# Shorter v loads with copies by VectorE, earlier transposing transfers, and more unread products at the start

## The chip, the cores and the metric

The kernel runs on one core of a Trainium2 chip. A core has a matrix engine (TensorE, PE in the profile), VectorE (DVE), ScalarE (ACT), GpSimd (POOL) and SyncE (SP), each with an instruction stream of its own that runs in order, and 16 DMA engines that they share. Matrix products write to PSUM, everything else lies in SBUF. The metric is the device time of one execution in microseconds; a time given for a kernel is the median of several runs, and a profile is one execution.

## The reference, cut to what matters

Chunked attention with a little memory, followed by a gated network. B, H, S, D = 4, 8, 768, 64; the queries of a sequence are cut into 24 chunks of 32, and each chunk sees 16 keys before it, its own 32, 8 after it and 8 memory keys.

```
for c in range(24):
    l, r = max(0, 32*c - 16), min(768, 32*c + 40)
    keys   = concat(mem_k, k[:, :, l:r]);  vals = concat(mem_v, v[:, :, l:r])
    s      = (q_c @ keys.T) / sqrt(64);    a = softmax(s)
    out[:, :, 32*c:32*c+32] = a @ vals
x = out.transpose(0, 2, 1, 3).reshape(3072, 512)
y = (maximum(x @ w_gate, 0) * (x @ w_val)) @ w_out      # d_ff = 1536
```

Inputs are float32 in DRAM, the result is 3072 x 512 float32. Inside, the kernel works in bf16 and f16.

## The kernel before, in words

**Tiles.** A tile is 128 queries of one batch (four chunks) with all eight heads: 24 tiles, six to a batch (`TPB`). The attention of tile a: transpose its q and k (L275, operations "t"), copy them out of PSUM ("tc"), scores (L309, 32 small products), row maximum and subtraction on VectorE, exponent on ScalarE, sum, reciprocal and normalisation on VectorE, transpose the probabilities (L358, "p") and copy them out ("pc"), then the products with the values (L388, "v"; L374 and L381 in batch 0) and a copy to xT ("x"). The network works on blocks of 2, 2, 2, 4, 4, 4, 4 and 2 tiles (`BLOCKS`): 12 pieces of w_gate and w_val (L407, "f"), ReLU on ScalarE (L413), product on VectorE (L419), then w_out (L432, "o") and a store.

**Transposes by transfer.** From tile `LATE_QK` on, q and k are transposed by DMA transfers that SP issues (L283); q lands in place, k in a buffer k_t that is then copied. From tile `LATE_P` on the same holds for the probabilities (L362). Both are 18 here, that is, batch 3.

**v.** In batch 0, v is loaded as it lies (v_n) and moved to the chunks' places by products with a shifted identity (L215, "sh") and copies. For the other batches v_bd[b % 2] holds, for each of 4 head pairs and 24 chunks, a 128 x 128 matrix: two heads on the diagonal, for each 56 rows of context and 8 of memory. So v_bd must be zero off the diagonal. Its context rows are loaded straight from DRAM with a cast (`load_v_rows`, L184): row s of chunk c is key 32c + s - 16, so 56 rows for each chunk, and the rows 32 to 55 of a chunk are the rows 0 to 23 of the next one, loaded a second time. Two loads a batch, one for each half of the heads; the last one of batch 3 is cut in two. The memory rows are copied in by small DMAs ("mr", L167), by SP in batch 1 and by GpSimd after. v_bd[1] is zeroed at the start by VectorE and ScalarE ("z1"). Parts of v_bd[0] serve batch 0 as v_q and vmem_f; it is zeroed by GpSimd ("z", L135), in the queue of its loads, after the values of tile 5.

**GpSimd** issues all casting loads in one fixed order (the list `loads`): q and k pairs and v of batch 0, weights, then the q and k tiles and v of later batches, mr among them.

**The order of the work** is made by a planner in the kernel (`schedule`). Each operation has engines with planned durations, dependencies, a priority, and buffers that it takes and gives; the planner steps through planned time and writes down one list, and each engine then runs its part of it in order. FFN evictions have priority 0, attention 1, network products on PE 2. `pace` and `pace_t` hold transposes of later tiles back.

**Unread products.** From planned 1.3 to `WARM` = 16 us, whenever PE has nothing ready, the planner puts in a product of zeros that nobody reads (`idle_product`, L140), planned at 0.107 us up to 6 us and 0.056 after. It writes to a buffer of the pool `fps` (four PSUM buffers, used by shifts and by the network), which is given back at planned 16.1 us. The scores take their PSUM tile anew for each tile from `sps`, a pool of one buffer.

Of the kernel before, what the change touches and what calls it, by code (L numbers as in the profile page):

```python
# [9 lines left out]
F32 = mybir.dt.float32  # L10
# [4 lines left out]
ACT = mybir.ActivationFunctionType  # L15
# [4 lines left out]
def kernel(  # L20
# [12 lines left out]
    nc = tc.nc  # L33

    B, H, S, D = q.shape
# [15 lines left out]
    BLOCKS = [2, 2, 2, 4, 4, 4, 4, 2]  # L51
    GROUPS = [(0, 2), (2, 6), (6, 9), (9, 12)]
    BAND0 = 48

    LATE_QK, LATE_P = 18, 18

    KEY_RUNS = ((0, CH, 0), (KW, 64, CH), (CH, KW, CTX))
    assert sum(BLOCKS) == NT and NMEM == 8 and D == 64 and H == 8
# [67 lines left out]
            moe_w_out.rearrange("(c p) f -> p c f", p=128)[:, n * i:n * i + n, :],  # L126
        )

    def zero(eng, t, hp):
        x = t[:, hp].bitcast(F32)  # L130
        if eng is nc.scalar:
            z = idle.bitcast(F32)
            nc.scalar.copy(x, bass.AP(tensor=z.tensor, offset=z.offset, ap=[z.ap[0], [0, NCH], [1, D]]))
        else:
            eng.memset(x.rearrange("p c d -> p (c d)"), 0.0)  # L135

    def idle_product(N):
        if "idle" not in TMP:
            TMP["idle"] = fps.tile([128, 512], F32, tag="fps", name="idle_ps")
        nc.tensor.matmul(TMP["idle"][:, 0:N], lhsT=idle, rhs=idle[:, 0:N], start=True, stop=True)  # L140


    def mem_load():
# [45 lines left out]
    def v_parts(b, par, c0, c1):  # L189
        parts = []  # L190
        if (b, par, c1) == (B - 1, 1, HP * NCH):
            c1 -= 1
            parts.append((b, par, 0, 48, c1, c1 + 1))
        return parts + [(b, par, 0, CTX, c0, c1)]


    def load_v_tile(t):
# [98 lines left out]

    def scores(a):
        b, t = divmod(a, TPB)
        s = sps.tile([128, 2, 512], F32, name="s_ps")
        keys = kT[b].rearrange("p h c s -> p h (c s)")  # L300
        for h2 in range(HP):
            m, par = h2 % 2, h2 // 2
            for g in range(4):
                c = 4 * t + g
                lo, hi = max(KW * c - 16, 0), min(KW * c + 48, NCH * KW)
                o0 = 64 * (2 * m + par) + lo - (KW * c - 16)
                for r in range(2):
                    d = slice(D * r, D * r + D)
                    nc.tensor.matmul(s[CH * g:CH * g + CH, r, o0:o0 + hi - lo],  # L309
                                     lhsT=qT[b][d, h2, CH * c:CH * c + CH],  # L310
                                     rhs=keys[d, h2, lo:hi], start=True, stop=True)
        S_ps[a] = s.rearrange("p a (h s) -> p a h s", s=64)[:, :, 0:HP, :]
# [155 lines left out]
    op("idle", {"DVE": 0.2}, lambda e: nc.vector.memset(idle, 0.0), prio=(-10,))  # L468
    for hp in range(HP):
        op(("z1", hp), {"DVE": 1.5, "ACT": 1.6}, lambda e, hp=hp: zero(engine[e], v_bd[1], hp), ["idle"], prio=(-1, hp), after=["warm2", "vmem_f"] + ["ib"] * (hp > 0))  # L470
    op("warm", {"DVE": 0.15}, lambda e: nc.vector.memset(warm, 0.0), prio=(-9,))  # L471
    op("warm2", {"ACT": 1.5}, lambda e: nc.scalar.activation(warm, warm, ACT.Exp), ["warm"], prio=(-9,))
    op("vmem_f", {"DVE": 0.55}, lambda e: nc.vector.memset(vmem_f, 0.0), prio=(-8,), after=["warm"])
# [42 lines left out]
    for a in range(NT):  # L516
# [41 lines left out]
        if b == 0:  # L558
# [46 lines left out]
    def load_qk_op(a, i):  # L605
        load(("qk", a, i), 1024, 1.05, lambda: load_qk(a, i), take=["qk"])

    def load_v_op(b, half, par, c0, c1, n, deps, after):
        for i, part in enumerate(reversed(v_parts(b, par, c0, c1))):
            rows = part[3] - part[2]  # L610
            load(("vl", b, half, n) if i == 0 else ("vx", b, n), rows * (part[5] - part[4]),
                 rows * (part[5] - part[4]) * 1.15e-3, lambda part=part: load_v_rows(*part), deps, (), after)
# [6 lines left out]
    def load_zero(s, hp):  # L619
        load(("z", s, hp), 0, 1.5, lambda: zero(nc.gpsimd, v_bd[s], hp), [("v", TPB - 1)])  # L620

    def load_pair_op(r, i):
        load(("pl", r, i), 1024, 1.45, lambda: load_pair(r, i))
# [25 lines left out]
    for i in range(2):  # L649
        load(("wo", i), 768, 4.1, lambda i=i: load_out(i))  # L650
    for b in range(1, B):
        deps = ([("z", 0, HP - 1)] if b > 1 else [("z1", hp) for hp in range(HP)]) + ([("v", TPB * (b - NSET + 1) - 1)] if b > NSET else [])
        if b == 1:
            for n in range(2 * HP):
                op(("mr", b, n), {"SP": 0.72}, lambda e, n=n: mem_rows(nc.sync, 1, n),
                   deps + [(("vm", 0), 0.2), (("vm", 1), 0.2)], (0,))
        for par in range(2):
            load_v_op(b, 0, par, 0, HP * NCH, par, [], deps)
# [12 lines left out]
    def timed(d):  # L671
        return isinstance(d, tuple) and len(d) == 2 and isinstance(d[1], float)
# [1 line left out]
    def schedule():  # L674
        done, started, times = {}, set(), [0.7]
        free = {e: 0.7 for e in ("PE", "ACT", "DVE", "SP", "POOL")}
        queue_end, flying, gives = 0.0, [], [(WARM + 0.1, "fps")]
        room["fps"] -= 1
        heapq.heappush(times, WARM + 0.1)
# [26 lines left out]
        while len(started) < len(ops) + len(loads):  # L706
# [8 lines left out]
            while moved:  # L715
                moved = False
                for e in ("POOL", "PE", "ACT", "DVE", "SP"):
                    if free[e] > t + 1e-9:
                        continue
                    if e == "POOL":  # L720
                        if n_load == len(loads):
                            continue
                        o = loads[n_load]
                        if len(flying) >= 8 or not ready(o, t):
                            continue
                        n_load += 1
                        key = o["key"]
                        if o["n"]:
                            end = t + 0.62 + 0.27e-3 * o["n"]
                            queue_end = max(queue_end, end + 0.8) + o["work"]  # L730
                            flying.append(queue_end + 1.0)
                            done[key] = queue_end + (1.2 if n_load < 8 else 2.4 if n_load < 45 else 6.0 if key[0] == "vl" else 4.0)
                        else:
                            end = done[key] = t + max(o["work"], 0.6)
                        fn = o["fn"]
                    else:
                        o = None
                        for _, key in todo[e]:
# [4 lines left out]
                            alone = len(ops[key]["eng"]) == 1 or e == "ACT"  # L743
                            if e != "PE" and 6.0 < t < HASTE and alone and ready(ops[key], t + 0.4):
                                break
# [70 lines left out]
```

## Time and profile before

| | |
|---|---|
| median of 3 runs | 248.03 us (247.85 to 248.07) |
| the profiled execution | 248.07 us |
| its span, first to last instruction | 246.3 us |
| mean granted TensorE clock | 0.993 |
| busy PE, DVE, ACT, POOL | 238.8, 139.8, 115.9, 85.4 us |
| first network product begins | 24.09 us |
| unread products | 138, the last ending at 16.9 us |
| v loads of batches 1 to 3 (L184) | 7 issues, 13.9 us of POOL, 17.3 us from issue to landing in the middle |
| zeros by GpSimd | 4 of 1.42 us, from 75.2 us |
| transposing transfers by SP | 18, from 109.98 us |

How to read it: a row of a view names the line of the kernel, the engine, what it writes and reads, and how often, then busy time and mean duration. "[0.87 <-issue]" behind an instruction of the timeline says that its engine sat idle 0.87 us before it, and what ended that; "issue" means that the profile shows nothing that it waited for. Matmuls overlap each other, so the spacing of two starts says more than a duration. A line number such as L78 or L80 is that of a helper that copies for many operations. The DMA share is of 16 engines and can exceed 1 where transfers overlap.

### The profile page before, as it was taken

Reading aid. Unit: us, or ns where it says so; the run is one execution under the profiler, and the core shown is the slowest. Engines: PE = TensorE matmul, PEld = TensorE weight load, DVE = VectorE, ACT = ScalarE, POOL = GpSimd, SP = SyncE. Lnnn points to the kernel's source line nnn. Section 1 sums busy time; section 2 is a strip of 40 time slices with the busy share of each in tenths; the row PEclk is TensorE's granted clock in tenths of the full one; section 3 lists DMA queues with packets and bytes.
Section 4 is the critical chain, followed back from the end, with each engine's and each line's share of the span. In section 5 each row is a group of like instructions: output and inputs, shape, how many; then the busy total and the mean of one; then the engine's idle time right before and its main releaser. Section 6 shows DMA issues by size and latency. Waiting matters only on the chain.

```text
span 246.3 us, 6675 instructions
## 1 busy us (share of the span) xinstructions
PE 238.8 (97%) x2811; PEld 146.5 (59%) x2811; DVE 139.8 (57%) x271; ACT 115.9 (47%) x259; POOL 85.4 (35%) x101
## 2 busy tenths in 40 slices
PE   7988998999999999999999999999999999999994
PEld 7776887886579645555445545455445444444873
DVE  5475868886278438796048779999342034320430
ACT  5665545754466334643235575765332232312432
POOL 8975689305289950398901420000000000000000
PEclk9998999999999999999999999999999999999999
DMA  7999999999999699399999594361101210002102
GB/s 75 174 180 204 201 158 184 175 138 84 168 202 135 37 159 130 26 132 141 181 198 144 24 109 85 110 148 27 21 3 45 85 43 0 0 33 97 43 3 85
DMA packets 109757, 25.77 MB, mean 105 GB/s; under 512 B 100768, under 2 KB 106656, under 8 KB 109728
## 3 DMA queue, kind: packets, MB, share of 16 engines
q0 software_dynamic: 94368, 16.42, 105.2%
q10 hardware_dynamic: 3600, 6.29, 7.5%
q1 hardware_dynamic: 11760, 2.64, 7.4%
q8 instruction: 22, 0.36, 0.6%
q14 instruction: 7, 0.06, 0.1%
HBM read 32.06 MB, written 6.29 MB: 156 GB/s over the span
## 4 chain that ended last, share of the span: by engine, by line
PE 93%; ACT 2%; issue 2%; DVE 1%; POOL 1%; ACTq 0%; DVEq 0%; POOLq 0%
PE v_ps L407 25%; PE out_ps L432 25%; PE g_ps L407 25%; PE xT_ps L388 3%; PE idle_ps L140 3%; PE s_ps L309 2%; PE qk_ps L275 2%; PE pT_ps L358 2%; PE vs_ps L215 2%; PE xT_ps L381 2%; PE qk_ps L236 1%; ACT kT L78 1%; PE xT_ps L374 1%; POOL qk_p L227 1%; ACT v_bd L78 0%
## 5 line engine op out<-in xcount | busy, mean ns | idle before, releaser
L419 DVE TENSOR_TENSOR gvT<-v_ps,g_relu 128x256 f16<-128x256 f32 (+1 forms) x96 | 52.9, 554 | 54.8 <-PE v_ps L407 40.7
L407 PE MATMUL v_ps<-xT,w_val_sb 128*128 128x256 f16 (+1 forms) x384 | 78.5, 327 | 0.1
L407 PE MATMUL g_ps<-xT,w_gate_sb 128*128 128x256 f16 (+1 forms) x384 | 78.5, 327 | 0.0
L413 ACT ACTIVATE g_relu<-g_ps 128x256 f16<-128x256 f32 (+1 forms) x96 | 46.9, 490 | 55.6 <-PE g_ps L407 53.7
L432 PE MATMUL out_ps<-w_out_sb,gvT 128*128 128x512 f16 (+2 forms) x300 | 65.8, 371 | 0.0
L407 PEld LDWEIGHTS <-w_gate_sb 128*128 128x128 f16 x384 | 36.8, 98 | 24.1 <-issue 0.4
L407 PEld LDWEIGHTS <-w_val_sb 128*128 128x128 f16 x384 | 35.9, 98 | 21.2 <-issue 0.3
L432 PEld LDWEIGHTS <-gvT 128*128 128x128 f16 x300 | 28.0, 98 | 29.7
L78 ACT COPY o_sb<-out_ps 128x512 f32<-128x512 f32 (+2 forms) x25 | 14.2, 568 | 34.4 <-PE out_ps L432 26.3
L337 ACT ACTIVATE p_exp<-dif 128x256 f16<-128x256 f32 (+2 forms) x72 | 19.6, 339 | 9.5 <-DVE dif L329 9.4
L254 POOL DMA_DIRECT2D qk_b<-in_k_dram x18 | 16.4, 909 | 18.6 <-issue 9.9
L167 POOL DMA_DIRECT2D v_bd<-vmem x16 | 10.1, 638 | 27.9 <-DMA v_bd<-in_v_dram 18.3
L322 DVE TENSOR_REDUCE mx<-s_ps 128x8 f32<-128x512 f32 x24 | 16.5, 689 | 5.4 <-PE s_ps L309 5.0
L341 DVE TENSOR_REDUCE sm<-p_exp 128x8 f32<-128x512 f16 x24 | 16.3, 680 | 4.2 <-ACT p_exp L337 4.1
L329 DVE TENSOR_TENSOR dif<-s_ps,mx 128x512 f32<-128x512 f32 x24 | 16.5, 686 | 0.4
L254 POOL DMA_DIRECT2D qk_b<-in_q_dram x18 | 16.3, 906 | 1.1 <-PE qk_ps L275 0.5
L352 DVE TENSOR_TENSOR p_n<-p_exp,rinv 128x512 f16<-128x512 f16 x24 | 16.5, 686 | 0.3
L78 ACT CAST xT<-xT_ps 128x512 f16<-128x512 f32 x16 | 9.4, 585 | 11.6 <-PE xT_ps L388 8.8
L184 POOL DMA_DIRECT2D v_bd<-in_v_dram x7 | 13.9, 1997 | 1.9 <-issue 1.0
L388 PEld LDWEIGHTS <-v_bd 128*128 128x128 f16 x288 | 9.6, 96 | 3.6
L140 PE MATMUL idle_ps<-idle 128*128 128x128 bf16 x138 | 10.7, 240 | 1.0 <-DVE warm L471 1.0
L80 DVE COPY qT<-qk_ps 128x512 bf16<-128x512 bf16 x9 | 4.1, 455 | 11.9 <-PE qk_ps L275 11.8
(57 smaller groups left out, 177.2 us busy)
## 6 DMA issues: line engine op xcount, KB each, us to landing
out_dram<-o_sb ACTq DMA_DIRECT2D x23, 256.0 KB
v_bd<-in_v_dram POOLq DMA_DIRECT2D x5, 672.0 KB, 17.3
qk_b<-in_k_dram POOLq DMA_DIRECT2D x18, 128.0 KB, 7.1
qk_b<-in_q_dram POOLq DMA_DIRECT2D x18, 128.0 KB, 7.0
w_out_sb<-in_moe_w_out_dram POOLq DMA_DIRECT2D x2, 768.0 KB, 10.6
qk_p<-in_k_dram POOLq DMA_DIRECT2D x3, 256.0 KB, 5.4
qk_p<-in_q_dram POOLq DMA_DIRECT2D x3, 256.0 KB, 6.7
v_n<-in_v_dram POOLq DMA_DIRECT2D x6, 128.0 KB, 6.4
```

What stands on the lines that cost most here:

```text
L78: nc.scalar.copy(o, i)
L140: nc.tensor.matmul(TMP["idle"][:, 0:N], lhsT=idle, rhs=idle[:, 0:N], start=True, stop=True)
L254: nc.gpsimd.dma_start(qk_b[a, i], bass.AP(tensor=x.tensor, offset=x[b, 0, 128 * t, 0].offset, ap=[[D, 128], [S * D, H], [1, D]]))
L322: nc.vector.reduce_max(SM[a, "mx"], s4, axis=AX.X)
L329: nc.vector.tensor_tensor(out=SM[a, "dif"].rearrange("p (m r) a s -> p r m a s", r=2), in0=S_ps.pop(a).rearrange("p r (m a) s -> p r m a s ...
L337: nc.scalar.activation(p[:, :, :, s0:s0 + k1 - k0], dif[:, :, :, k0:k1], ACT.Exp, scale=SCALE)
L352: nc.vector.tensor_tensor(out=P_n[a], in0=SM.pop((a, "p")), in1=rinv_b, op=ALU.mult)
L388: nc.tensor.matmul(ps[:, hp, r], lhsT=v_bd[b % NSET][:, hp, 4 * t + g, :], rhs=x[:, hp, r], start=True, stop=True)
L407: nc.tensor.matmul(ps, lhsT=w[:, f, 128 * m:128 * m + 128], rhs=xTs[blk][:, f, :], start=(f == 0), stop=(f == NFC - 1))
L413: nc.scalar.activation(st["r", m], st.pop((0, m)), ACT.Relu)
L419: nc.vector.tensor_tensor(out=st["gv"][:, m, :], in0=st.pop((1, m)), in1=st.pop(("r", m)), op=ALU.mult)
L432: nc.tensor.matmul(st["o", t, c], lhsT=st["gv"][:, m, 128 * t:128 * t + 128], rhs=w_out_sb[:, m, c[0]:c[1]], start=(m == 0), stop=(m == ND ...
```

## The change

- The two v loads of a batch read 32 rows for each chunk instead of 56 ("vl"), and one more small load for each half of the heads brings the last 16 rows behind the last chunk ("ve"). Rows 32 to 55 of a chunk are copied on VectorE from rows 0 to 23 of the next chunk (`upper`, "up"): 24 partitions by at most 12 chunks of 64, eight copies for each three tiles (`UT`), 16 a batch, 48 in all. The values of tile t of a batch wait for the copies up to its third.
- The zeros of v_bd[0] are made by ScalarE or VectorE ("z0"): one head pair at the start, after v_bd[1]'s, and the other three in thirds of eight chunks; that of the last pair after vmem_f has been read, the two that hold v_q after the values of tile 5.
- `LATE_QK` and `LATE_P` go from 18 to 15: q, k and probabilities of tiles 15, 16 and 17 are transposed by transfers too, and their issue is held back by `pace_t`.
- Unread products fill planned gaps up to 22 us, planned at 0.107 us up to 9 us and 0.060 after. They write into an unused part of the second bank of the score tile, which is now one tile for the whole kernel, and no buffer of `fps` is held for them.

```diff
+    UT = 3
-    LATE_QK, LATE_P = 18, 18
+    LATE_QK, LATE_P = 15, 15
...
+    s_all = sps.tile([128, 2, 512], F32, name="s_ps")
     def idle_product(N):
-        if "idle" not in TMP:
-            TMP["idle"] = fps.tile([128, 512], F32, tag="fps", name="idle_ps")
-        nc.tensor.matmul(TMP["idle"][:, 0:N], lhsT=idle, rhs=idle[:, 0:N], start=True, stop=True)
+        nc.tensor.matmul(s_all[:, 1, 256:256 + N], lhsT=idle, rhs=idle[:, 0:N], start=True, stop=True)
...
+    def upper(b, par, i0, i1, eng):
+        x = v_bd[b % NSET].rearrange("p h c d -> p (h c) d")
+        d = slice(D * par, D * par + D)
+        copy(eng, x[64 * par + CH:64 * par + CTX, i0:i1, d], x[64 * par:64 * par + CTX - CH, i0 + 1:i1 + 1, d])
...
+    op(("z0", HP - 2), {"DVE": 1.5, "ACT": 1.6}, ..., ["idle"], prio=(-1, HP), after=["ib", ("z1", 0)])
+    for hp in (HP - 1, 0, 1):
+        for c0 in range(0, NCH, 8):
+            op(("z0", hp, c0), {"ACT": 0.6, "DVE": 0.55}, lambda e, hp=hp, c0=c0: zero(engine[e], v_bd[0], hp, c0, c0 + 8),
+               ["vm0" if hp == HP - 1 else ("v", TPB - 1)], prio=(3, -hp) if hp == HP - 1 else (0.7, hp), after=[("v", 3)])
...
-           + ([("vl", b, 0, n) for n in range(2)] if b else [("shc", 4 * t), ("shc", 4 * t + 2), "vm0"])
+           + ([("vl", b, n) for n in range(2)] + [("up", b, n, m) for n in range(2 * HP) for m in range(t // UT + 1)]
+              + [("ve", b, n) for n in range(2) if last] if b else [("shc", 4 * t), ("shc", 4 * t + 2), "vm0"])
...
+    def load_v_op(b, par, deps):
+        n = HP * NCH
+        load(("vl", b, par), CH * n, CH * n * 1.03e-3, lambda: load_v_rows(b, par, 0, CH, 0, n), (), (), deps)
+        load(("ve", b, par), 16, 0.05, lambda: load_v_rows(b, par, CH, CH + 16, n - 1, n), (), (), deps)
+    for b in range(1, B):
+        for n in range(2 * HP):
+            hp, par = divmod(n, 2)
+            for m in range(TPB // UT):
+                i0 = NCH * hp + 4 * UT * m
+                i1 = min(i0 + 4 * UT, HP * NCH - 1)
+                op(("up", b, n, m), {"DVE": 0.1 + 64 * 0.5e-3 * (i1 - i0)}, ...,
+                   [("vl", b, par)], (1, TPB * b - 1 + UT * m, 9), (), (), [("v", TPB * b - 7)] if b > 1 else [])
...
-        if b == 1:
-            for hp in range(HP):
-                load_zero(0, hp)
-    HASTE, WARM = 0.0, 16.0
+    WARM = 22.0
...
-        queue_end, flying, gives = 0.0, [], [(WARM + 0.1, "fps")]
-        room["fps"] -= 1
+        queue_end, flying, gives = 0.0, [], []
...
-                                free[e] = t + (0.107 if t < 6.0 else 0.056)
+                                free[e] = t + (0.107 if t < 9.0 else 0.06)
```

More of the change, by code (lines that the diff above doesn't have):

```diff
@@ L127, in load_out, with zero @@
         )
[L129 to L130 removed]
+    def zero(eng, t, hp, c0=0, c1=NCH):
+        x = t[:, hp, c0:c1].bitcast(F32)
         if eng is nc.scalar:
             z = idle.bitcast(F32)
[L133 removed]
+            nc.scalar.copy(x, bass.AP(tensor=z.tensor, offset=z.offset, ap=[z.ap[0], [0, c1 - c0], [1, D]]))
         else:
             eng.memset(x.rearrange("p c d -> p (c d)"), 0.0)
+    s_all = sps.tile([128, 2, 512], F32, name="s_ps")
     def idle_product(N):
[L138 to L140 removed]
+        nc.tensor.matmul(s_all[:, 1, 256:256 + N], lhsT=idle, rhs=idle[:, 0:N], start=True, stop=True)
     def mem_load():
@@ L298, in scores @@
         b, t = divmod(a, TPB)
-        s = sps.tile([128, 2, 512], F32, name="s_ps")
+        s = s_all
         keys = kT[b].rearrange("p h c s -> p h (c s)")
@@ L470 @@
         op(("z1", hp), {"DVE": 1.5, "ACT": 1.6}, lambda e, hp=hp: zero(engine[e], v_bd[1], hp), ["idle"], prio=(-1, hp), after=["warm2", "vmem_f"] + ["ib"] * (hp > 0))
+    op(("z0", HP - 2), {"DVE": 1.5, "ACT": 1.6}, lambda e: zero(engine[e], v_bd[0], HP - 2), ["idle"], prio=(-1, HP), after=["ib", ("z1", 0)])
+    for hp in (HP - 1, 0, 1):
+        for c0 in range(0, NCH, 8):
+            op(("z0", hp, c0), {"ACT": 0.6, "DVE": 0.55}, lambda e, hp=hp, c0=c0: zero(engine[e], v_bd[0], hp, c0, c0 + 8),
+               ["vm0" if hp == HP - 1 else ("v", TPB - 1)], prio=(3, -hp) if hp == HP - 1 else (0.7, hp), after=[("v", 3)])
     op("warm", {"DVE": 0.15}, lambda e: nc.vector.memset(warm, 0.0), prio=(-9,))
@@ L606, in load_qk_op @@
         load(("qk", a, i), 1024, 1.05, lambda: load_qk(a, i), take=["qk"])
[L608 to L612, printed above, removed]
+    def load_v_op(b, par, deps):
[8 more added lines that the diff above has]
+                i1 = min(i0 + 4 * UT, HP * NCH - 1)
+                op(("up", b, n, m), {"DVE": 0.1 + 64 * 0.5e-3 * (i1 - i0)},
+                   lambda e, b=b, par=par, i0=i0, i1=i1: upper(b, par, i0, i1, engine[e]),
+                   [("vl", b, par)], (1, TPB * b - 1 + UT * m, 9), (), (), [("v", TPB * b - 7)] if b > 1 else [])
     def load_w_op(g):
@@ L651 @@
     for b in range(1, B):
-        deps = ([("z", 0, HP - 1)] if b > 1 else [("z1", hp) for hp in range(HP)]) + ([("v", TPB * (b - NSET + 1) - 1)] if b > NSET else [])
+        deps = ([("z0", HP - 2)] + [("z0", hp, c0) for hp in (HP - 1, 0, 1) for c0 in range(0, NCH, 8)] if b > 1 else [("z1", hp) for hp in range(HP)]) + ([("v", TPB * (b - NSET + 1) - 1)] if b > NSET else [])
         if b == 1:
@@ L657 @@
         for par in range(2):
[L658 removed]
+            load_v_op(b, par, deps)
         if b > 1:
@@ L742, in schedule @@
                                 break
-                            alone = len(ops[key]["eng"]) == 1 or e == "ACT"
-                            if e != "PE" and 6.0 < t < HASTE and alone and ready(ops[key], t + 0.4):
-                                break
                         if o is None:
```

9 lines of the change are left out of this document (removed).

## The prediction

> **What bounds the kernel now.** I read the page's busy shares first, then its slices, the chain of waits, a table of windows, and last the instructions of PE in order of time.
>
> ```profile
> span 246.3 us, 6675 instructions
> PE 238.8 (97%) x2811; PEld 146.5 (59%) x2811; DVE 139.8 (57%) x271; ACT 115.9 (47%) x259; POOL 85.4 (35%) x101
> PEclk9998999999999999999999999999999999999999
> PE 93%; ACT 2%; issue 2%; DVE 1%; POOL 1%; ACTq 0%; DVEq 0%; POOLq 0%
> q8 instruction: 22, 0.36, 0.6%
> ```
>
> TensorE sets the end: 93% of the chain is its own work, and from 46 us on it waits for nobody. So a product removed after 46 us is worth its spacing, and whatever VectorE, ScalarE, GpSimd or the DMAs gain is worth nothing by itself. The fourth digit of the clock row is an 8: in the slice from 18.5 to 24.6 us the granted clock is down. The windows show how much (columns: stretch, length, busy time of PE, weight load, DVE, ACT, POOL, granted clock, DMA share, GB/s).
>
> ```profile
> 18.76:22.18 3.42, 2.55 (x105) 1.96 (x106) 1.62 (x4) 1.65 (x3) 1.87 (x4) 1.00 1.25 202
> 22.18:25.59 3.41, 3.41 (x46) 2.68 (x41) 2.47 (x5) 2.41 (x6) 1.79 (x3) 0.50 1.27 203
> 39.24:42.65 3.41, 2.70 (x62) 2.10 (x61) 3.37 (x6) 1.41 (x4) 3.41 (x3) 1.00 1.31 199
> ```
>
> A window in which PE was busy 2.55 of 3.42 us (75%) is followed by one at half clock in which PE never idles. Half of 3.41, 1.70 us, is lost there. The window with 2.70 (79%) had no such follower.
>
> Why was PE idle in the first? In order of time (start, length, instruction):
>
> ```profile
> 14.05 0.22 PE L309 MATMUL s_ps<-kT,qT 64*32 64x64 bf16 x7 [0.40 <-issue]
> 14.20 0.85 PE L215 MATMUL vs_ps<-v_n,band 128*64 128x256 f16 x12
> 14.98 1.91 PE L140 MATMUL idle_ps<-idle 128*128 128x128 bf16 x31
> 16.82 0.41 PE L236 MATMUL qk_ps<-ident_b,qk_p 128*64 128x128 bf16 x8
> 17.16 0.40 PE L358 MATMUL pT_ps<-band,p_n 128*128 128x128 f16 x4
> 18.05 0.41 PE L236 MATMUL qk_ps<-ident_b,qk_p 128*64 128x128 bf16 x8 [0.49 <-ACT qT L78]
> 18.40 0.40 PE L374 MATMUL xT_ps<-pT,vmem 128*128 128x128 f16 x4
> 18.73 0.68 PE L381 MATMUL xT_ps<-pT,v_bd 56*64 56x32 f16 x32
> 19.34 0.40 PE L358 MATMUL pT_ps<-band,p_n 128*128 128x128 f16 x4
> 19.66 0.26 PE L309 MATMUL s_ps<-kT,qT 64*32 64x64 bf16 x18
> 20.80 0.25 PE L309 MATMUL s_ps<-kT,qT 64*32 64x64 bf16 x14 [0.87 <-issue]
> ```
>
> Both "issue" stops fall in the middle of a tile's scores and wait for no engine. Between them lie 7+12+31+8+4+8+4+32+4+18 = 128 products, with their weight loads 256 instructions. The instruction queue moved 0.36 MB in 22 pieces, 16 KB each, which is 64 bytes for each of 256. So I read them as waits for the next block of PE's program. Blocks came 6.75 us apart here (14.05 to 20.80) while the DMAs are full: 53 ns a product.
>
> **The change part by part.**
>
> *Transposes of tiles 15 to 17.* PE loses three times the q and k transposes (eight products; 137.59 to the next one at 138.04: 0.45 us) and the transpose of P (153.62 to 153.84: 0.22). 3 x 0.67 = 2.0 us off the bound engine, about 125 to 155 us. Six evictions go (0.42 on DVE or 0.59 on ACT), three k copies stay, now from k_t (0.29 or 0.61). SP issues nine more transposing transfers, 1.19 to 1.31 us each, 11 us; it has nothing between its rows for v_bd, which end at 46.7, and 109.98. The q and k ones go ahead of tile 18's. Those of P are new among the q and k transfers of tiles 21 to 23 (144.10 to 153.2 now): a late q or k load holds SP, P of tile 15 stands behind it, and PE at tile 15's values behind that. Bounds: nothing, as for tiles 18 to 21, where P was ready at 155.97 and used at 161.40 with PE not waiting; up to 3.8 us, SP's longest wait for p_n. I take nothing, since tiles 18 to 21 are the same step.
>
> *v loads.* Each batch's two loads shrink from 56 to 32 rows of 96 chunks, 5376 to 3072 pieces, plus two of 16 pieces. POOL takes 2.2 us for 5376 and 0.9 for the 1024 of a q tile, so 1.5 for 3072 and 0.6 for a small one (24 KB rows of v_bd: 0.63): 4.2 us a batch against 4.4. The DMAs get some 13,700 of 94,368 packets less; PE waits for no DMA after 46 us, so: nothing.
>
> *Copies instead.* 48 on VectorE, up to 12x64 elements. The row nearest is the copy kT<-kmemT, 768 elements too, 0.30 to 0.33 us: 48 x 0.33 = 16 us. They lie ahead of the values of tiles 6, 9, 12, 15, 18 and 21. Cover: VectorE is idle 4.3 us in 55 to 65 us, 3.1 in 90 to 110, and PE has other work, since values of tile 13 end at 117.8 and the block that needs them begins at 124.16; tile 17's end at 156.3, its block begins at 162.78. Some 6 us at each. Cost nothing; without the cover, 5.3 us a batch.
>
> *Zeros.* POOL loses four fills of 1.42 us at 75.2 to 80.6, which held the loads behind them. DVE or ACT gain one of 1.34 or 1.46 near the start and nine thirds (512 f32 elements: 0.49 us by the fill at 1.03 us). The first fits ScalarE's hole of 2.35 us before 7.34; if it slips behind, up to 1.46 us at the start. Three come at some 35 us, six behind the values of tile 5 at 53.9, where VectorE is busy 3.01 of 5 us. Nothing taken.
>
> *Unread products.* They now fill planned gaps up to 22 instead of 16, write into a spare part of the score tile, and free one of four PSUM buffers at the start (shifts may run earlier; up to 0.4 us, not taken). The planner's 16 is about 16.9 in the trace. PE's own work from there to 22.9 takes about 4.3 us of 6.0, so up to 28 products of 0.06 us are added; the thinner spacing up to 9 and 0.060 for 0.056 takes away about 16 of the 77 issued from 6.9 to 16.9 and just before. Net about +12 of 138. Two effects, opposite:
> - More products keep PE busy in the window before the clock falls. It lacked 0.15 us to the 2.70 that kept full clock; three added products. Gain 1.70 us if the window clears, nothing if not.
> - Each costs program: 12 x 53 ns = 0.6 us while blocks bind. Bounds 0 (they fill waits for data, such as the 0.49 at 17.5) and 28 x 0.06 = 1.7 us. I take 0.6.
>
> The Trainium skill ("TensorE: Matmul & The Clock Gate", Part 1, on oscillation) puts the danger at idle gaps above about 3.4 us. The longest gap here is 0.87 us and the clock fell, so here the share of a window decides; by the rule as written, the added products could not matter, and the time would be that of the second case below.
>
> Sum against the profiled execution (span 246.3, time 248.07, 1.77 around it; the median is 248.03): 246.3 - 2.0 - 1.7 + 0.6 = 243.2, and with 1.77: 245.0 us.
>
> **The rivals.**
>
> *The clock falls all the same.* The stop at 20 us is for program, which added products cannot fill and may lengthen. For it: the window's idle time was nearly all that stop. Against: the count of products before 16 falls too, which moves where the block ends. 245.0 + 1.7 = 246.7.
>
> *Slower: the start starves.* If the added products are used up before the block of 20 us arrives, real work waits behind them: 28 x 0.056 = 1.6 us later, and the window's busy share falls well below 75%, so a second half-clock window follows, 1.7 more. 248.07 - 2.0 + 3.3 = 249.4. It decides from a loss of 2.0 us at the start, before the first product of the network (24.09 now). Against it: the planner places them only where it sees PE idle.
>
> *The copies wait for GpSimd.* One row of the copy kT<-kmemT is far off the rest:
>
> ```profile
> L263 DVE COPY kT<-kmemT x4: 297/330/1790, 7.4 to 137.8; 128x768 bf16<-128x768 bf16 x4
> 38.07 4.43 POOL L184 DMA_DIRECT2D v_bd<-in_v_dram  x2 [0.42 <-DVE gvT L419]
> ```
>
> It ran from 38.67 to 40.46, while POOL wrote the first v load (half of 4.43: to 40.29); alone it takes 0.33. If each copy at 90 to 112 waits out a q or k load of 0.9 us, sixteen cost 16 x 1.2 = 19 us against 3.1 + 6.2 of room, and the network stalls some 10 us: about 255 us; it costs from a mean of 0.58 us a copy on, and loses to before from 0.77 on. Against: the same copy ran 0.30 at 7.38 and 0.35 at 85.62 beside POOL's loads of 0.6. The Trainium skill ("SBUF — State Buffer", on the shared port pair) says that such a copy and a GpSimd operation shut each other out for a whole instruction; one row agrees, two do not.
>
> **How the numbers follow.** First case 0.45 (own range 243.4 to 246.0: without the 0.6 and with the 0.4 and 0.49 of the start, or with the 1.7), clock falls all the same 0.28, starved start 0.16, copies locked out 0.07; 0.04 for no change, gains and stalls cancelling. Faster (by over 0.2%, 0.5 us, about what a measurement can tell) 0.73, within 0.04, slower 0.23. The range 243.4 to 248.9 leaves out the lock, part of the starved start, and the low tail.
>
> **What would show it.** Right: clock full from 6 us on; 36 products fewer at L275 and L358 and PE still without waits after 46 us; first network product before 23.5 us. Wrong: a half-clock window after 18 us; "issue" stops longer than 0.87 us; VectorE copies into v_bd of over 0.6 us; a wait of PE at the values of tiles 15 to 17 for a transposing transfer.

## The result, and the profile after

The changed kernel takes 247.13 us (median; 246.28 to 248.35) against 248.03 us for the kernel before beside it (247.05 to 254.2): a ratio of 0.9964, with a 95% interval of 0.9949 to 0.9980. So it is faster by 0.9 us, where 3.0 were forecast (245.0); the time lies inside the range of 243.4 to 248.9. Ratios, here and below, leave out executions more than 1.5% above the fastest of their kernel; medians take all of them. Both kernels were profiled twice, since the first profile of the changed one is of the slowest of its 20 executions (248.35 us); the lines below are of the second, an execution of 247.65 us (span 245.9). From its page:

```profile
span 245.9 us, 6706 instructions
PE 237.8 (97%) x2789; PEld 145.4 (59%) x2789; DVE 153.7 (63%) x313; ACT 121.0 (49%) x269; POOL 77.7 (32%) x102
PEclk9999999999999999999999999999999999999999
PE 91%; DVE 4%; issue 2%; DMA 1%; ACT 0%; SPq 0%; ACTq 0%
L81 DVE COPY v_bd<-v_bd 24x768 f16<-24x768 f16 (+1 forms) x48 | 17.3, 399 | 1.3 <-DMA v_bd<-in_v_dram 0.7
```

The clock row is clean, as forecast. TensorE has 22 products less (36 transposes gone, 14 unread products added), and VectorE 13.9 us more. In the chain of waits VectorE now has 4%, where it had 1%. All waits of PE, from the table of waits (columns: for what, us in total, times, longest):

```profile
PE s_ps L141 <- DVE dif L329: 1.6, 2, 0.8
PE s_ps L309 <- issue: 1.3, 1, 1.3
PE s_ps L141 <- DVE warm L476: 1.0, 1, 1.0
PE kmem_ps L154 <- DMA kmem_f<-in_mem_k_dram: 0.7, 1, 0.7
PE s_ps L141 <- DVE mx L322: 0.4, 2, 0.2
```

None of them lies after 30 us; the first profile has one there, 0.46 us at 69.9 for the probabilities that VectorE normalises (L352). The first and the last are unread products that wait for VectorE; before, once they ran, they waited for nobody. In the order of time on PE:

```profile
13.16 0.27 PE L141 MATMUL s_ps<-idle 128*128 128x128 bf16 x2 [0.20 <-DVE mx L322]
14.21 1.17 PE L141 MATMUL s_ps<-idle 128*128 128x128 bf16 x18 [0.78 <-DVE dif L329]
15.31 0.31 PE L309 MATMUL s_ps<-kT,qT 64*32 64x64 bf16 x32
...
16.55 0.77 PE L141 MATMUL s_ps<-idle 128*128 128x128 bf16 x11 [0.15 <-DVE mx L322]
18.10 1.72 PE L141 MATMUL s_ps<-idle 128*128 128x128 bf16 x28 [0.78 <-DVE dif L329]
...
25.63 0.61 PE L407 MATMUL g_ps<-xT,w_gate_sb 128*128 128x256 f16 x4
26.07 0.60 PE L407 MATMUL v_ps<-xT,w_val_sb 128*128 128x256 f16 x4
26.51 0.60 PE L407 MATMUL g_ps<-xT,w_gate_sb 128*128 128x256 f16 x4
27.04 0.28 PE L309 MATMUL s_ps<-kT,qT 64*32 64x64 bf16 x23
28.65 0.23 PE L309 MATMUL s_ps<-kT,qT 64*32 64x64 bf16 x9 [1.33 <-issue]
```

The tile that they write is the one that the row maximum and the subtraction read, and although no column is shared, each waits for the other: PE 0.78 us twice, with the scores of tile 1 queued behind, and VectorE's subtraction 0.36 and 0.27 us. The first product of the network comes at 25.63 us, not before 23.5. Then comes a stop of 1.33 us that waits for no engine, in the middle of a tile's scores like the two before; the prediction read these as waits for PE's program, and the section on the half-clock window shows that they are.

Where the time lies is best seen from the starts of the network's blocks (first g_ps product of each in the trace, us):

| | block 0 | block 2 | block 4 | block 6 | end of span | time |
|---|---|---|---|---|---|---|
| before | 24.1 | 69.4 | 124.2 | 196.2 | 246.3 | 248.07 |
| before, second profile | 24.9 | 70.2 | 125.0 | 197.0 | 247.1 | 248.87 |
| changed, first profile | 25.6 | 71.5 | 126.5 | 196.5 | 246.6 | 248.35 |
| changed, second profile | 25.6 | 70.7 | 125.8 | 195.8 | 245.9 | 247.65 |

From block 4 to block 6, where tiles 15 to 17 lie, the changed kernel takes 70.0 us and the kernel before 72.0, each of them in both profiles. Those are the 2.0 us forecast. The start is 0.7 to 1.5 us later, and nothing was gained there.

### The profile page after: what moved, and what is told of

Its sections match the earlier page's. It is cut to its first block, busy times and chain, and to the rows that moved or that the text cites. A ratio compares the mean times of both kernels' runs of the same rounds, so it can differ in the third digit from the quotient of the medians.

```text
span 246.6 us, 6706 instructions
## 1 busy us (share of the span) xinstructions
PE 237.7 (96%) x2789; PEld 145.2 (59%) x2789; DVE 154.4 (63%) x313; ACT 121.0 (49%) x269; POOL 77.5 (31%) x102
## 3 DMA queue, kind: packets, MB, share of 16 engines
q0 software_dynamic: 76128, 14.65, 82.1%
## 4 chain that ended last, share of the span: by engine, by line
PE 93%; DVE 3%; DMA 1%; issue 1%; ACT 0%; SPq 0%; ACTq 0%
PE v_ps L407 26%; PE g_ps L407 26%; PE out_ps L432 24%; PE s_ps L141 4%; PE xT_ps L388 3%; PE s_ps L309 2%; PE qk_ps L275 2%; PE qk_ps L236 2%; PE pT_ps L358 2%; PE xT_ps L381 1%; PE vs_ps L215 1%; DMA kmem_f<-in_mem_k_dram 1%; PE xT_ps L374 1%; DVE mx L322 1%; DVE dif L329 1%
## 5 line engine op out<-in xcount | busy, mean ns | idle before, releaser
L413 ACT ACTIVATE g_relu<-g_ps 128x256 f16<-128x256 f32 (+1 forms) x96 | 47.2, 493 | 52.4 <-PE g_ps L407 51.1
L81 DVE COPY v_bd<-v_bd 24x768 f16<-24x768 f16 (+1 forms) x48 | 18.0, 415 | 2.7 <-DMA v_bd<-in_v_dram 2.1
L352 DVE TENSOR_TENSOR p_n<-p_exp,rinv 128x512 f16<-128x512 f16 x24 | 16.5, 686 | 0.4
L141 PE MATMUL s_ps<-idle 128*128 128x128 bf16 x152 | 13.4, 254 | 3.0 <-DVE dif L329 1.6
L185 POOL DMA_DIRECT2D v_bd<-in_v_dram x12 | 11.0, 924 | 9.9 <-DVE dif L329 9.2
L141 PEld LDWEIGHTS <-idle 128*128 128x128 bf16 x152 | 11.6, 116 | 4.1 <-issue 2.4
```

What stands on the lines that cost most here:

```text
L81: eng.tensor_copy(o, i)
L141: nc.tensor.matmul(s_all[:, 1, 256:256 + N], lhsT=idle, rhs=idle[:, 0:N], start=True, stop=True)
L352: nc.vector.tensor_tensor(out=P_n[a], in0=SM.pop((a, "p")), in1=rinv_b, op=ALU.mult)
L413: nc.scalar.activation(st["r", m], st.pop((0, m)), ACT.Relu)
```

## The experiments

Ratios are against runs of the kernel before on the same chip (247.8 to 248.1 in the middle), with 95% intervals. "The v part" is the shorter loads, the copies and the moved zeros together.

**The transposes, and what they need.** First the changed kernel without them, then the kernel before with them alone.

```diff
 after_late18 (the changed kernel)
-    LATE_QK, LATE_P = 15, 15
+    LATE_QK, LATE_P = 18, 18
 only_late15 (the kernel before)
-    LATE_QK, LATE_P = 18, 18
+    LATE_QK, LATE_P = 15, 15
```

> The kernel after with the transposing transfers from tile 18 again. Theory 1: the 2.0 us of the transposes come back in full, 249.1, ratio to before 1.0045. Rival: the transposes are worth less beside the loaded VectorE, 247.1 to 248.

> The kernel before with the transposing transfers from tile 15 alone; v loads and zeros as before. Theory 1: 36 products fewer and PE still without waits after 46 us, 246.0, ratio 0.992. Rival 4, the transfers need the room that the shorter v loads make: PE waits at tiles 15 to 17, 248 or more.

Without them the changed kernel takes 248.85 us, 1.0030 (1.0013 to 1.0046): against 0.9964 they are worth 0.66%, 1.6 us. But alone they make the kernel before slower: 251.01 us in the middle of all executions, a ratio of 1.0085 (1.0049 to 1.0121). Its table of waits and PE's order of time:

```profile
PE xT_ps L388 <- DMA pT<-p_n: 3.3, 1, 3.3
148.17 0.59 PE L388 MATMUL xT_ps<-pT,v_bd 128*128 128x32 f16 x16 [3.30 <-DMA pT<-p_n]
```

The values of a tile wait for the transposing transfer of its probabilities. SP issued it at 138.79, at once after p_n (138.08 to 138.76), so SP was not held; PE could go on at 148.17, 9.4 us later. The windows tell why (columns as in the prediction), here of only_late15:

```profile
134.00:138.00 4.00, 4.00 (x95) 2.05 (x83) 4.00 (x8) 3.27 (x9) 0.00 (x0) 1.00 3.11 135
138.00:142.00 4.00, 4.00 (x21) 1.75 (x19) 3.90 (x9) 1.70 (x3) 0.63 (x1) 1.00 4.64 101
146.00:150.00 4.00, 1.83 (x20) 0.98 (x20) 0.58 (x1) 1.21 (x4) 3.79 (x5) 0.64 1.38 102
```

and of the changed kernel:

```profile
134.00:138.00 4.00, 4.00 (x67) 2.14 (x64) 3.62 (x7) 2.96 (x8) 0.00 (x0) 1.00 0.69 68
138.00:142.00 4.00, 4.00 (x57) 1.82 (x54) 3.90 (x10) 2.31 (x7) 0.00 (x0) 1.00 0.07 12
```

With 56-row loads the DMA share is 3.11 and 4.64: batch 3's loads of v, issued at 113 to 121, take up to 26.5 us to land and lie across the transfers. With 32-row loads (up to 10.2 us to landing) the DMAs are nearly empty there. After the wait the clock is down too (0.64, and 0.51 from 150 to 154). So the gain of the transposes needs the shorter loads. The half of the step that has no such transfer, q and k alone:

```diff
-    LATE_QK, LATE_P = 18, 18
+    LATE_QK, LATE_P = 15, 18
```

> Before with q and k of tiles 15 to 17 transposed by transfers, P of these tiles still by TensorE (LATE_QK 15, LATE_P 18). If the loss of the full step made alone (1.0085) came from P's transfers standing behind q's and k's on SP, this gains 3 x 0.45 = 1.35 us: 0.9945, with no wait of PE above 0.3 us after 60 us. If q's and k's transfers are late themselves, PE waits at the copies or scores of tile 15, near 140 us, and the ratio is 1.00 or above.

It has no long wait any more (0.17 us at 150.8), and blocks 4 to 6 take 71.0 us, 1.0 less than before; the time is 248.18 us, 1.0003 (0.9972 to 1.0035). The profiled execution (247.29 us) is 0.8 us below that of before. That P's transfers are what lost is shown. The 1.35 us that q's and k's were to gain are not there in the time: 0.9945 lies below the interval. The trace has 1.0 us less in blocks 4 to 6, and why the median shows none of it stays open.

**The v part, and what it costs.** The kernel before with `upper`, `load_v_op` and the "z0" operations of the diff above (and the score tile taken once, as in the change); then the zeros alone; then loads and copies alone, GpSimd still writing its zeros. In short:

```diff
 only_v          + upper, load_v_op, ("z0", ...); - load_zero      (WARM 16, LATE 18)
 only_zeros      + ("z0", ...); - load_zero                        (56-row loads)
 only_copies     + upper, load_v_op                                (load_zero stays)
```

> The kernel before with the 32-row v loads, the copies on VectorE and the moved zeros alone (products, transposes as before). Theory V, this part costs what the transposes gained with it (2.0 less the 0.3 that the two showed together): 249.7, with PE waits between 55 and 105 us. Rival as predicted, it is hidden: 248.0.

> Before with the zeros of v_bd[0] alone moved from GpSimd to ScalarE and VectorE. The v part as a whole costs 0.53% of before (248.90 against 247.8), and this takes it apart. Theory Z (the zeros cost it, because they take 4.4 us of VectorE and ScalarE between 35 and 60 us and one fill of 1.4 us at the start): ratio 1.004 to 1.006. Theory C (the loads and copies cost it): 1.000 within 0.0015. Theory P (it is a matter of where PE's program blocks fall, and any shift of the start costs as much as another): between, 1.001 to 1.004, with the longest issue stop between 20 and 60 us longer than 0.87.

> Before with 32-row v loads and the 48 copies on VectorE; GpSimd still writes the zeros. Theory Z: ratio 1.000 within 0.0015. Theory C (copies of 0.4 us make evictions of the network and the values late; or the earlier loads take DMA time from PE's program): 1.004 to 1.006. Theory P: 1.001 to 1.004. If both this and the zeros alone come out at 1.000, the two cost only together.

The whole v part: 248.90 us, 1.0053 (1.0040 to 1.0066). The zeros alone: 247.95 us, 1.0011 (0.9982 to 1.0040), not told from nothing. Loads and copies without the moved zeros: 256.21 us in the middle against 247.88, a ratio of 1.034 of the medians; five of its six executions lie between 255.35 and 257.89, one at 248.28, like the whole v part. None of the theories had that. VectorE and PE of only_copies, from an execution of 256.36 us, in the order of time:

```profile
65.94 6.84 DVE L81 COPY v_bd<-v_bd 24x768 f16<-24x768 f16 x1
72.81 0.20 DVE L347 RECIPROCAL rinv<-sm 128x8 f32<-128x8 f32 x1
73.43 0.69 DVE L354 TENSOR_TENSOR p_n<-p_exp,rinv 128x512 f16<-128x512 f16 x1
74.18 0.61 PE L360 MATMUL pT_ps<-band,p_n 128*128 128x128 f16 x4 [5.59 <-DVE p_n L354]
```

and GpSimd:

```profile
65.46 0.89 POOL L256 DMA_DIRECT2D qk_b<-in_q_dram  x1
66.32 0.90 POOL L256 DMA_DIRECT2D qk_b<-in_k_dram  x1
67.18 5.38 POOL L136 MEMSET v_bd<- 128x1536 f32 x4
72.86 1.45 POOL L187 DMA_DIRECT2D v_bd<-in_v_dram  x1 [0.30 <-POOL v_bd L136]
```

A copy that takes 0.35 us (the median of the 48) took 6.84: it began while GpSimd made a load, and ended at 72.78, 0.2 us after the last of four fills that followed without a gap. p_n was late by that, PE stood 5.59 us, and two windows at half clock followed (72.9 to 79.7). That is the third rival of the prediction, in the fills and not in the loads. The Trainium skill ("SBUF — State Buffer", on the shared port pair) says that a VectorE copy of this kind and a GpSimd operation shut each other out for a whole instruction; this run agrees, and in it back-to-back GpSimd instructions were waited out as one. Moving the zeros off GpSimd is therefore worth about 7 us beside the copies where a copy meets the fills (1.034 against 1.0053 in the medians), and nothing without the copies. That the four other long executions met them too is likely and not shown, as one execution was profiled; the one of 248.28 shows that it is not certain to happen.

Does the same lock, behind loads, make the rest of the 0.5%? The v part profiled again, and with its copies on ScalarE:

```diff
 v_act (only_v)
-                op(("up", b, n, m), {"DVE": 0.1 + 64 * 0.5e-3 * (i1 - i0)}, ...
+                op(("up", b, n, m), {"ACT": 0.1 + 64 * 0.9e-3 * (i1 - i0)}, ...
```

> The v part alone, profiled again, since its first profile was of the fastest of five executions (247.81; the others 248.84 to 249.61). Expected 248.8 to 249.6; the cost shows either before the first product of the network (start later than 24.1 us) or as waits of PE between 55 and 105 us beyond the 0.40 and 0.17 seen before (network block 2 to block 4 longer than 55.2 us).

> The v part alone (32-row loads, copies, zeros off GpSimd; 1.0053), with the 48 copies on ScalarE instead of VectorE. If the copies' waiting for GpSimd's instructions on VectorE (13 of 48 stretched from 0.35 to 0.45 to 1.05 us, 4.5 us in all) is what the v part costs, this comes out at 1.000 to 1.002 although a copy takes ScalarE 0.8 to 0.9 us. If the cost is the extra work ahead of the network's evictions, or where program blocks fall, it stays at 1.004 or above.

Run again, the v part takes 248.66 us, 1.0039 (1.0001 to 1.0076), and its profile shows one such place. The rows of VectorE, PE and GpSimd:

```profile
68.61 3.77 POOL L187 DMA_DIRECT2D v_bd<-in_v_dram  x4
69.04 1.18 DVE L81 COPY v_bd<-v_bd 24x704 f16<-24x704 f16 x1
70.25 0.42 DVE L81 COPY pT<-pT_ps 128x512 f16<-128x512 f16 x1
70.72 0.38 PE L277 MATMUL qk_ps<-ident_b,qk_b 128*128 128x128 bf16 x4 [0.52 <-DVE pT L81]
```

The copy at 69.04 ends at 70.22, 0.15 us after the first of the four load instructions (68.61 to 70.07 in the trace); the copy of P behind it is late, and PE waits 0.52 us. Besides, a stop for program of 0.26 us at 57.9 (0.40 in the first profile). With both, 0.6 to 0.8 us of the 1.0 to 1.3 are located: blocks 2 to 4 take 55.2 and 55.5 us in these two profiles, and 54.8 in both of the kernel before. The rest stays open. Copies on ScalarE are no way out: 252.92 us, 1.0200 (1.0153 to 1.0248). Each takes 0.82 us there, 37.5 us in all, and PE then waits for xT, kT and g_relu, 0.9 us at most at a time.

**The unread products.** The change's products in the kernel before; the change with the products of before; the change with its products in a buffer of their own.

```diff
 only_idle       (before)   + s_all, WARM 22, 0.107 to 9 us and 0.060 after
 idle_as_before  (changed)  - WARM = 22.0   + WARM = 16.0, fps buffer, spacing as before
 idle_apart      (changed)  - nc.tensor.matmul(s_all[:, 1, 256:256 + N], ...
                            + nc.tensor.matmul(TMP["idle"][:, 0:N], ...      # fps buffer, held to planned 22.1
```

> The kernel before with the unread products of the change alone (score tile, to 22 us). Theory 1: the start loses what the change lost there, 247.1 + 2.0 = 249.1, ratio 1.004; the waits of PE for row maximum and subtraction are there and no half-clock window after 18 us. Rival 3: the start is neutral or better, 247 to 248.

> The kernel after with the unread products of before altogether (buffer of fps, to 16 us, old spacing). Both theories of the start: the half-clock window and the program stops of before are back, and the 2.0 us of the transposes stand alone: 246.0, ratio 0.992. Rival 3, the copies on VectorE and the moved zeros eat the gain of the transposes: 247.1 or more.

> The kernel after, with the unread products written to a buffer of fps (held to planned 22.1 us) and no longer to the score tile; the order of PE's instructions is that of the kernel after. Theory 1, the shared score tile ties the products to VectorE's row maximum and subtraction (PE waits 0.3 to 0.8 us four times there, VectorE 0.36 and 0.27 for the products): those waits go, the first network product moves from 25.63 to about 24 us, and the time falls by some 1.5 us to 245.6, ratio to before about 0.990. Rival 2, the number and place of the products cost what the start lost: 247.1 as after, ratio 0.996.

In the kernel before they cost: 248.58 us, 1.0032 (1.0015 to 1.0049). The change without them takes 247.38, 0.9988 (0.9960 to 1.0015), and with them apart 247.23, 0.9978 (0.9951 to 1.0006); both overlap the changed kernel's interval. So beside the other parts they are worth between nothing and 0.6 us. Why they lose alone and not there stays open. With the buffer apart, the waits for VectorE are gone and the network begins at 23.3 us; but then the same program block is late by more:

```profile
PE s_ps L311 <- issue: 2.4, 1, 2.4
PE vs_ps L217 <- issue: 0.5, 1, 0.5
```

and a window at half clock follows (26.96 to 30.38). In this execution, what one wait gives, the next takes.

**The half-clock window.** Both kernels again, unchanged.

> The kernel before, unchanged, profiled again. Most of its executions show a mean clock of 0.998 or more, that is, no half-clock window, at the same time. If the window of 22 to 26 us costs its 1.70, an execution without it has its fourth block of the network start 1.7 us earlier than 124.2. If the fourth program block (product 479) holds PE there anyway, an issue stop of some 1 to 1.7 us stands at 24 to 26 us in its place and block 2 starts at 69.0 to 69.5 as before.

> The changed kernel, unchanged, profiled again: its first profile was of an execution of 248.35, at the slow end. Expected 246.5 to 247.3, with the tile-15-to-17 stretch (block 4 to block 6) at the same 70.0 us, and the difference before 60 us: shorter or fewer of the issue stops of 0.78, 0.78 and 1.49.

The kernel before took 247.94 us (0.9999, 0.9966 to 1.0033), the changed one 247.39 (0.9969, 0.9933 to 1.0004). The second profile of before has no half-clock window, and a stop that the first has not:

```profile
26.28 0.31 PE L309 MATMUL s_ps<-kT,qT 64*32 64x64 bf16 x32
26.52 0.52 PE L215 MATMUL vs_ps<-v_n,band 128*64 128x256 f16 x5
28.34 0.41 PE L215 MATMUL vs_ps<-v_n,band 128*64 128x256 f16 x4 [1.31 <-issue]
```

Its first q transposes began 1.86 us later than in the first profile (8.75 against 6.89). At the scores of 26.2 the two are level (26.22 and 26.28): the full clock had made that up. Behind the stop, at the 479th product, it is 1.6 late again (26.75 and 28.34). The cleanest pair is the v part alone, whose two profiles have the same order on PE, first without the window,

```profile
6.55 0.64 PE L238 MATMUL qk_ps<-ident_b,qk_p 128*64 128x128 bf16 x16
24.27 0.31 PE L311 MATMUL s_ps<-kT,qT 64*32 64x64 bf16 x32
24.51 0.52 PE L217 MATMUL vs_ps<-v_n,band 128*64 128x256 f16 x5
26.34 0.62 PE L217 MATMUL vs_ps<-v_n,band 128*64 128x256 f16 x7 [1.31 <-issue]
26.90 0.40 PE L360 MATMUL pT_ps<-band,p_n 128*128 128x128 f16 x4
```

then with it (22.37 to 25.78):

```profile
6.97 0.64 PE L238 MATMUL qk_ps<-ident_b,qk_p 128*64 128x128 bf16 x16
26.09 0.31 PE L311 MATMUL s_ps<-kT,qT 64*32 64x64 bf16 x32
26.34 1.04 PE L217 MATMUL vs_ps<-v_n,band 128*64 128x256 f16 x12
27.31 0.40 PE L360 MATMUL pT_ps<-band,p_n 128*128 128x128 f16 x4
```

The starts are 0.42 us apart (6.55 and 6.97). At the scores the one at full clock leads by 1.82. It then stops at its 479th product for 1.31, and at the transposes of P the two are 0.41 apart again. The instruction queue (q8 of the DMA view, window by window) shows what the stop waits for: the 16 KB piece of program behind it began to arrive at 23.91 us in the first profile and at 24.30 in the second, 0.39 apart like the starts. Every stop of this kind before 30 us, in all profiles of these experiments, ended 2.2 to 2.7 us after such a piece had begun. So the window costs nothing here: whether PE gets to the end of its program block at full or half speed, the next block comes at the same time.

The other executions bear this out by their mean granted clock (one window makes 0.993). Of those of the kernel before that the ratios use, 25 lie below 0.997, with a median of 247.88 us, and 92 above, with 247.87. And none of the 12 executions of only_idle has a window, which is slower than the kernel before all the same.

**Less program.** 128 columns of zeros per unread product against 256 and 512: the same time on PE planned, with 54 products instead of 138 (or 152), 168 (or 196) of PE's instructions less ahead of the network. In the kernel before, in the change with the products apart, and in the change with the products of before (best_wide).

```diff
-                                order.append((t, lambda: idle_product(128)))
+                                order.append((t, lambda N=256 if t < 9.0 else 512: idle_product(N)))
```

> The kernel before, with its unread products two to four times as wide (256 columns up to planned 9 us, 512 after), so 54 instead of 138 for about the same busy time; the order of the rest on PE is unchanged. Theory P, PE waits for its next 256 instructions: 168 instructions fewer, the stops that wait for nothing at 13.7 (0.40) and 19.9 us (0.87) go, with them the half-clock window (1.70), and the time falls by 1.3 to 3.0 us: 245.0 to 246.7. Rival, these stops have another cause and stay at the same place in the scores: 248.0.

> The kernel after, its unread products in a buffer of fps and two to four times as wide, 54 instead of 152. Theory P with theory 1: no wait for VectorE, no stop for program (2.43 us at 25.0 with narrow products there), no half-clock window, first network product before 24 us: 247.2 - 2.4 = 244.8 or less. Rival: the start is bound by data, 247.

> The v part and the transposes of tiles 15 to 17 as in the changed kernel, unread products as before in time but 256 and 512 columns wide (54 instead of 138, so 84 products or 168 instructions less of PE's program ahead of the network). If PE's start is paced by its program blocks alone and fewer products free it, 245.5 to 246.5 (0.990 to 0.994). If the stops only move to a later block, as with the wide products in the kernel before (0.9994 against 1), this equals the same kernel with narrow products, 247.4: 0.996 to 1.000.

In the kernel before it takes 247.61 us, 0.9994 (0.9973 to 1.0016). The network begins at 22.2 us instead of 24.1, but block 2 at 69.5 as before: the stops are now for later blocks,

```profile
PE v_ps L408 <- issue: 0.8, 1, 0.8
PE xT_ps L382 <- issue: 0.7, 1, 0.7
```

at 23.0 and 51.5 us, with a half-clock window behind the second (52.4 to 55.8). The first stop falls at the same count of products as the one of 20 us in the kernel before, with network products on both sides where scores were: the count decides, and not the work. In the change with products apart: 247.79, 0.9980 (0.9951 to 1.0009). In best_wide the network begins at 22.1, and two executions at full clock took 245.47 and 246.29; the other four have windows at half clock and took 248.58 to 250.20. Its median is 248.89, against 248.14 beside it, so it is no better kernel; the ratio of 0.9889 (0.9821 to 0.9957) rests on three of the six.

Here, unlike above, a lower clock and a longer time go together. So they do in two others whose half-clock window lies later than the one of 22 us: with products apart (27 to 30 us in the profiled execution) the four executions below 0.997 that the ratio uses are at 248.48 in the middle and the seven above at 246.60; with products apart and wide (56 to 60 us) six are at 248.31 and four at 246.06. No stop for program stands behind these windows to take the loss up. That is the likely reason and not shown: where the window lay is known for one execution of each, and in the first kernel of the next pair five executions with windows are no slower (246.99) than five without (247.66).

Last, the copies put where there is room, with narrow and with wide products:

```diff
-                op(("up", b, n, m), {"DVE": 0.1 + 64 * 0.5e-3 * (i1 - i0)}, ...
+                op(("up", b, n, m), {"DVE": 0.1 + 64 * 0.5e-3 * (i1 - i0), "ACT": 0.1 + 64 * 0.9e-3 * (i1 - i0)}, ...
```

> Transposes of tiles 15 to 17 and the v part, unread products as before (0.9988 with all copies on VectorE), each copy on VectorE or ScalarE as the planner finds room. If the lock on VectorE is the cost: 0.994 to 0.996. If not: 0.998 to 1.000.

> The same, and each copy on VectorE or ScalarE as the planner finds room. With narrow products this made 0.997 against 0.9988 (intervals overlap). If VectorE's lateness between 55 and 105 us is a cost of its own, this is lower than the one above by 0.001 to 0.003; if not, the two are equal within 0.0015.

They take 247.16 us, 0.9970 (0.9936 to 1.0005), and 248.34 us, 0.9984 (0.9949 to 1.0020). The first equals the changed kernel; nothing here beats it reliably.

## Why the prediction was off, point by point

*What bounds the kernel.* Right, and not taken far enough. PE sets the end and waits for program at the start; both were read from the profile. But the two were added as if apart.

*Clock, -1.7.* This is the step that failed, and the largest of the misses. The window cleared, as forecast (none of the changed kernel's 28 executions has a mean clock below 0.998), and brought nothing: the same block of 128 products that the prediction used to price an unread product stands behind the window and holds PE until it comes (pairs of profiles above). The first network product was to come before 23.5 us and came at 25.63. The rival "the clock falls all the same" has the nearest time (246.7), for another reason: the clock did not fall. The cause given for the window falls as well. In the changed kernel two windows, one before and one after the network's first product (columns as in the prediction; their edges are counted back in steps of 3.413 us from the fall of the clock at 245.47, after the last products),

```profile
13.37:16.78 3.41, 2.48 (x69) 2.09 (x67) 1.67 (x3) 2.43 (x7) 3.41 (x6) 1.00 1.80 181
27.02:30.43 3.41, 2.08 (x53) 1.62 (x53) 1.97 (x5) 1.92 (x6) 2.75 (x4) 1.00 1.32 200
```

have PE busy 73% and 61%, less than the 75% that was read as the danger, and no half clock follows. Busy share does not decide it. The rule weighed beside it (the Trainium skill, "TensorE: Matmul & The Clock Gate", Part 1: idle gaps above about 3.4 us) does not cover it either: ahead of the window of the kernel before the longest gap is 0.87 us, with the products apart 2.43. Where PE stood 5.59 us (copies alone) the clock fell too, as that rule has it. What decides in the others is open.

*Transposes of tiles 15 to 17, -2.0.* Right in the trace (72.0 to 70.0 us), 1.6 by the times. The bound for the new transfers of P, up to 3.8 us, was nearly met when they were made alone (3.30), though not for the reason given: SP was free, the DMAs were full. "Nothing" was right only because the same change shortens the loads, and the prediction gave those no worth at all. (It put the packets saved at 13,700; the queue of these loads has 18,240 less, 76,128 for 94,368.)

*v loads 0, copies 0, zeros 0.* This is the second miss. Together +1.0 to +1.3 us by themselves, of which 0.6 to 0.8 are located: a copy that waited for GpSimd's load and made a P copy late, and a later stop for program. The copies take 399 to 415 ns in the changed kernel against 330 taken; the cover of 6 us before each block's values was counted, but not what else stands behind a copy on VectorE, here the copy of P out of PSUM that PE waits for. Costing the zeros at nothing fits the step by itself (1.0011, not told from nothing) and missed that it is what makes the copies affordable. The rival "copies wait for GpSimd" was given 0.07: its mechanism is real, its place was the fills, which the change removes.

*Unread products, +0.6.* The count was right (+14 for +12). What they cost came from elsewhere: waits on VectorE at the score tile, 0.78 us twice, which the prediction did not look for because no column is shared. Alone +0.8 us, beside the rest between 0 and -0.6.

*The sum by what was measured.* -1.6 for the transposes (left out of the change), +1.0 to +1.3 for the v part (alone in the kernel before), 0 to -0.6 for the products (left out of the change): between -1.2 and -0.3 us, around the -0.9 measured. PE has no waits after 30 us in the second profile, as forecast, and one of 0.46 us in the first. The start lost 0.7 to 1.5 us, near the 1.6 of the rival "the start starves", but by waits for VectorE, and no second half-clock window followed. Of the signs of being wrong two came, a stop of 1.33 us and copies of up to 0.85 us; a half-clock window after 18 us and a wait at the values of tiles 15 to 17 did not.

## What to carry to other kernels

A gain in front of a wait for something that comes at its own pace is worth nothing: before a slow window is priced at what it loses, look at what PE would have waited for next, here the next block of its program. Parts of a change that look free can be what another part stands on (shorter loads for the transfers, moved zeros for the copies), so ask of each whether a resource that it frees is one that another part needs. And where engines share a tile, read the waits at the tile and not at the columns.

## What the runs showed of the hardware

- PE's program came in 16 KB pieces, and in four profiles of this order (before, the v part, zeros alone, copies alone) the first five began 6.0 to 6.9 us apart (11.56, 18.34, 24.48, 30.77 and 37.03 in before) while the DMAs were full. The stops of PE with nothing to wait for, 0.2 to 2.5 us, fell at the 223rd, 351st, 479th or a later product by a multiple of 128, or up to five ahead; those before 30 us ended 2.2 to 2.7 us after a piece had begun. The Trainium skill ("Runtime: NRT & Kernel Launch", on instruction fetch) puts the cost of crossing such a block at "mostly hidden"; here it was not.
- A VectorE copy of 24 x 768 or 704 f16 in SBUF took 0.35 us in the median, 0.45 to 1.18 where GpSimd's making of a load held it, ending about 0.2 us after a load instruction, and 6.84 in front of four fills. In the profiles with these copies 7 to 13 of the 48 were stretched, and 12 to 23 others that overlapped a GpSimd instruction were not.
- With the DMA share at 3 to 4.6, the first product that needed a transposing transfer of 128 x 512 f16 ran 9.4 us after the issue.
